# Two fused layers in f32: three d_ff chunks in a step of the inner loop, across block borders, in place of two

## The chip, the cores and the metric

The kernel runs on one core of one Trainium2 chip. The metric is device time in microseconds (us), the median of several executions; lower is better. Five engines work side by side, each through its own instructions in order, and wait for each other through semaphores: TensorE (PE, matrix multiplication), VectorE (DVE), ScalarE (ACT), GpSimd (POOL) and SyncE (SP, which issues the DMA transfers here). Matmul results land in PSUM, which has eight banks of 512 f32 columns on each of 128 partitions; all else lies in SBUF.

## The reference

Attention through 49 agent vectors, then a layer with two weight matrices, both on 4 batches of 12480 tokens with 128 channels, in f32.

```python
def _attn_ref(q, k, v, agents):
    scale = 1.0 / np.sqrt(q.shape[-1])
    def sm(a, b):
        s = scale * (a @ b.transpose(0, 2, 1))
        s = s - s.max(-1, keepdims=True)
        e = np.exp(s)
        return e / (e.sum(-1, keepdims=True) + 1e-09)
    agent_v = sm(agents, k) @ v
    return sm(q, agents) @ agent_v

def _moe_ref(x, w_in, w_out):        # w_in 128 x 2048, w_out 2048 x 128
    h = x @ w_in
    g = h - np.tanh(h)
    return g @ w_out
```

## The kernel before

**What it computes.** For each batch, *phase 1* forms `agent_v` from keys and values (scores, maxima, exponentials, sums) and multiplies it by `w_in`. The product, 49 agents by 2048, is kept as a high and a low part (`awh`, `awl`) in the type f32r, in which a matmul takes one pass; a plain f32 matmul takes four. After that a block of 480 tokens needs only its 49 softmax weights, also split into two parts and transposed (`pT`, 98 rows). For small h, h - tanh(h) is computed as h times the square of tanh(0.775 h) with a constant at the end; a general path stands behind a branch that is not taken on this data.

**The inner loop.** The work is 104 blocks of 480 tokens (26 a batch) by 16 chunks of 128 of the 2048 d_ff columns. A *step* is one block and two chunks, so there are 832:

- `m1` (L398, L399): four f32r matmuls of 480 columns on PE, which write h into a PSUM tile of two banks. There are three h tiles (six banks) and two single banks (`misc`) for everything else.
- `act`: on ACT tanh y from h (L408), its square z (L410); on DVE g = h * z (L412). Each works on 960 columns at once.
- `high` (L442): POOL copies g to gh in f32r, its high part. `low` (L447): DVE subtracts, gl = g - gh, the low part.
- `m2`: three f32r matmuls a chunk add into the block's output: gh with the low part of `w_out` (L459), gh with its high part (L460), gl with its high part (L461).

In every second block the last pair is *plain*: g itself is multiplied with f32 weights `wo_f` (L457), with neither gh nor gl. That is 52 pairs.

**The order.** The code issues m1 of step s, its `act` and `high`, `low` of step s-1 and `m2` of step s-2. A scheduler then sorts the instructions of each engine by a timeline of its own, within the dependencies, before the program is built; on the chip each engine keeps that order.

**Background.** Beside the loop run generators, advanced once a step: for every pair of blocks the softmax of the next pair (`q_softmax`: matmuls L353, DVE L363, L370 to L373, POOL L366 and L378, ACT L364, L368, L376) and two transposes (`q_transpose`, L385, L390); in the first three batches phase 1 of the next batch (matmuls L228, L276 and L327, DVE L232, L290, L331, L333, POOL L264, ACT L231, L266). Results leave through `finish` (L522). Before the loop, phase 1 of the first batch and the decoding of the weights run alone. In the main part keys go through three buffers and values through four.

Of the kernel before, what the change touches and what calls it, by code (L numbers as in the profile page):

```python
# [44 lines left out]
PCUT = (0, 256, 768, 1280, 1792, 2048)  # L45
NP = 5
KV0 = 13
KV = 3
VB = 4
PLAIN_PAIR = NCH // 2 - 1  # L50
PLAIN_EVERY = 2
LAG1 = 1
LAG2 = 1
NB = dict(y=2, z=2, g=4, gh=3, gl=2)
# [18 lines left out]
class Build:  # L73
    def __init__(self, ctx, tc, aps):
        self.tc, self.nc = tc, tc.nc
        self.qT, self.kT, self.v, self.agT, self.wi, self.wo, self.outT = aps
        self.pool = lambda name, bufs=1, **kw: tc.tile_pool(name=name, bufs=bufs, **kw)
        self.const = ctx.enter_context(self.pool("const"))
        self.keep = ctx.enter_context(self.pool("keep"))
        self.small = ctx.enter_context(self.pool("small", 2))  # L80
        self.ph = ctx.enter_context(self.pool("ph", 3, space=PSUM))
        self.pmisc = ctx.enter_context(self.pool("pmisc", 2, space=PSUM))

    def begin(self, ctx, name):
        self.work = ctx.enter_context(self.pool(name, reuse_waits="tile"))

    def wtile(self, tag, bufs):
        return self.work.tile([128, 1024], F32, tag=tag, name=tag, bufs=bufs)
# [4 lines left out]
    def constants(self):  # L93
# [15 lines left out]
        self.wo_f = c.tile([128, 2, C], F32, tag="wo_f", name="wo_f")  # L109
        self.vb = [c.tile([128, GT, C + 2], F32, tag=f"v{i}", name=f"v{i}") for i in range(VB)]  # L110
        for vt in self.vb:
# [39 lines left out]
    def load_w_out(self, c, raw):  # L151
# [7 lines left out]
        if c == PLAIN_PAIR // 2:  # L159
            nc.scalar.copy(self.wo_f.rearrange("p n e -> p (n e)"), w[:, 2 * C * (PLAIN_PAIR % 2) :][:, : 2 * C])  # L160

    def phase1(self, b):
        nc = self.nc
        st = {}
        kb, vb = (KV0 if b == 0 else KV), VB
# [7 lines left out]
        def load_k(g):  # L173
            n = tiles(g)
            kt = self.work.tile([128, GT * 128], F32, tag="kv", name="kt", bufs=kb)
            kt = kt.rearrange("p (t n) -> p t n", n=128)[:, :n, :]
# [3 lines left out]
        def load_v(g):  # L180
            vt = self.vb[g % VB]
# [13 lines left out]
        def scores(g):  # L195
# [7 lines left out]
            kt = ahead("k", load_k, g, kb if b == 0 else kb - 1)  # L203
            if b and g >= NG - vb:
                ahead("v", load_v, 0, g - NG + vb + 1)
            if b == 0:
                ps = self.ph.tile([128, 2, 512], F32, tag="h", name="h")
# [50 lines left out]
        def av(g):  # L258
            vt = ahead("v", load_v, g, vb - 1)
# [8 lines left out]
            if b == 0:  # L268
                if g == 0:
                    st["ps"] = self.ph.tile([128, 2, 512], F32, tag="h", name="h")[:, 0, :]  # L270
# [39 lines left out]
    def project(self, b, bound):  # L310
        nc = self.nc

        def part(c, lo, hi):
# [8 lines left out]
            if b == 0 and bound:  # L322
                ps = self.ph.tile([128, 2, 512], F32, tag="h", name="h")[:, 0, :]
# [69 lines left out]
    def m1(self, aw, pT, i):  # L393
        nc = self.nc
        h = self.ph.tile([128, 2, 512], F32, tag="h", name="h")
        for c in range(2):
            sl = slice((2 * i + c) * 128, (2 * i + c + 1) * 128)
            nc.tensor.matmul(h[:, c, :BLK], aw[0][:A2, sl], pT[:A2], start=True, stop=False)  # L398
            nc.tensor.matmul(h[:, c, :BLK], aw[1][:A2, sl], pT[:A2], start=False, stop=True)  # L399
        return h  # L400

    def pair(self, t):
        return t[:, : 2 * BLK].rearrange("p (c n) -> p c n", c=2)

    def act(self, h):
        nc = self.nc
        y = self.pair(self.wtile("y", NB["y"]))
        nc.scalar.activation(y, h[:, :, :BLK], AF.Tanh, scale=TSC)  # L408
        z = self.wtile("z", NB["z"])[:, : 2 * BLK]
        nc.scalar.activation(z, y.rearrange("p c n -> p (c n)"), AF.Square)  # L410
        g = self.wtile("g", NB["g"])[:, : 2 * BLK]
        nc.vector.tensor_tensor(self.pair(g), h[:, :, :BLK], self.pair(z), ALU.mult)  # L412
        return g

    def act_general(self, h):
        nc = self.nc
        hv = h[:, :, :BLK]
        d = self.wtile("y", NB["y"])[:, : 2 * BLK]
        u = self.wtile("z", NB["z"])[:, : 2 * BLK]
        nc.scalar.activation(self.pair(d), hv, AF.Tanh)  # L420
        nc.scalar.activation(self.pair(u), hv, AF.Square)
        nc.vector.tensor_tensor(self.pair(d), hv, self.pair(d), ALU.subtract)
        big = self.wtile("y", NB["y"])[:, : 2 * BLK]
        nc.vector.tensor_scalar(big, u, 4.0, None, ALU.is_ge)
        nc.vector.tensor_scalar(u, u, 16.0, None, ALU.min)
        r = self.wtile("z", NB["z"])[:, : 2 * BLK]
        nc.vector.tensor_scalar(r, u, 1.0 / 15.0, 13.0, ALU.mult, ALU.add)
        g = self.wtile("g", NB["g"])[:, : 2 * BLK]
# [7 lines left out]
        nc.vector.tensor_tensor(self.pair(g), hv, self.pair(g), ALU.mult)  # L436
# [3 lines left out]
    def high(self, g):  # L440
        gh = self.wtile("gh", NB["gh"])[:, : 2 * BLK].bitcast(F32R)
# [3 lines left out]
    def low(self, g, gh):  # L445
        gl = self.wtile("gl", NB["gl"])[:, : 2 * BLK].bitcast(F32R)
# [3 lines left out]
    def m2(self, acc, i, gh, gl):  # L450
        nc = self.nc
        for c in range(2):
            f = 2 * i + c
            x = slice(c * BLK, (c + 1) * BLK)
            first, last = f == 0, f == NCH - 1
            if gl is None:
                nc.tensor.matmul(acc[:, :BLK], self.wo_f[:, c, :], gh[:, x], start=first, stop=last)  # L457
                continue
            nc.tensor.matmul(acc[:, :BLK], self.wo_l[:, f, :], gh[:, x], start=first, stop=False)  # L459
            nc.tensor.matmul(acc[:, :BLK], self.wo_h[:, f, :], gh[:, x], start=False, stop=False)  # L460
            nc.tensor.matmul(acc[:, :BLK], self.wo_h[:, f, :], gl[:, x], start=False, stop=last)  # L461

    def fast(self):
        nc, tc = self.nc, self.tc
        HP = NCH // 2
        blocks = [(b, j) for b in range(B) for j in range(NBLK)]
        steps = [(n, i) for n in range(len(blocks)) for i in range(HP)]
# [58 lines left out]
        def foreground(n, i):  # L526
            h = self.m1(self.aw[blocks[n][0]], pT[n][0], i)
            while done:
                finish(done.pop(0))
            return h  # L530

        def rest(n, i, h):
            g = self.act(h)
            even = n % PLAIN_EVERY == 0
            plain = even and i == PLAIN_PAIR
            gh = None if plain else self.high(g)
            q1.append((n, i, g, gh))

        def low(keep):
            while len(q1) > keep:  # L540
                n, i, g, gh = q1.pop(0)
                q2.append((n, i, g, None) if gh is None else (n, i, gh, self.low(g, gh)))

        def out(keep):
            while len(q2) > keep:
                n, i, gh, gl = q2.pop(0)
                if i == 0:
                    acc[n] = self.misc()
                self.m2(acc[n], i, gh, gl)
                if i == HP - 1:  # L550
                    done.append(n)

        for n, i in steps:
            b = blocks[n][0]
            pos = (n % 2) * HP + i
            p = n // 2
            if n % NBLK == 0 and i == 0 and b + 1 < B:
                kq = self.phase1(b + 1)
            h = foreground(n, i)
            if n == 0 and i < len(rest0):  # L560
                run(rest0[i])
# [8 lines left out]
            rest(n, i, h)  # L570
            low(LAG1)
            out(LAG2)
# [9 lines left out]
            if (pos + 2) % 16 in KS and kq and n % NBLK < 25:  # L582
                start(kq.pop(0))
        low(0)
# [3 lines left out]
    def general(self):  # L588
# [10 lines left out]
        with tc.If(bits > HMAX_BITS):  # L599
            for b in range(B):  # L600
                for t in self.project(b, False):
                    run(t)
                with tc.For_i(0, NBLK * BLK, GW) as at:
                    pp = run_value(self.q_softmax, b, self.q_load(self.qT[:, ds(b * N + at, GW)]))
                    o = self.work.tile([128, GW], F32, tag="out", name="o", bufs=2)
                    for half in range(2):
                        pT = run_value(self.q_transpose, pp, half)
                        acc = self.misc()
                        for i in range(NCH // 2):
# [34 lines left out]
```

## Time and profile before

| | |
|---|---|
| median of three runs | 2228.51 us (2228.47 to 2228.87) |
| span of the profiled execution | 2226.8 us |
| instructions in the span | 31246 |
| first m1 matmul (L398) | 86.6 us after the start |
| first g (L412) | 92.3 us after the start |
| matmul pieces L398, L399 | 1664 each |
| L459, L460, L461 | 1560 each |
| steps with gh and gl (L442, L447) | 780 of 832 |

The times of the profile come from one execution, recorded on the chip. A row of a group of instructions reads: line, engine, operation, output <- inputs by the program's names with their shapes, count | busy us in all, mean ns of one | idle time of the engine just before them, with what ended most of it. A row of a timeline reads: start in us, duration in us, engine, line, operation, names, shapes, count; in square brackets the idle time ahead and what ended it. Adjacent rows of one kind are merged (x2). Recorded durations of neighbours on one engine overlap a little, since an instruction starts while the one before it still writes; the spacing of starts is what an operation costs. A row of a stretch reads: from and to, length, busy time of each engine (instructions), granted TensorE clock, busy share of the DMA engines, GB/s.

### The profile page before, as it was taken

To read this page: it belongs to the slowest core of one execution; us is meant where nothing else is said; L and a number is where in the kernel's file an instruction comes from. 1 tells how busy PE (TensorE), PEld (TensorE's weight loads), DVE (VectorE), ACT (ScalarE), POOL (GpSimd) and SP (SyncE) were. 2 spreads that over 40 slices of the span, in tenths; PEclk is the share of its full clock that TensorE was granted. 3 is DMA by queue.
4 is the path that set the end of the run, shared out by engine and by line. 5 is a ranking of instruction groups with operands and counts; after the bars stand their busy time and mean duration, and the time that the engine had idled before them with its cause. 6 is when DMAs were issued, how large, how long until landed. Compare 5 with 4: busy or idle time off the path is not lost.

```text
span 2226.8 us, 31246 instructions
## 1 busy us (share of the span) xinstructions
PE 2181.5 (98%) x11083; PEld 1838.3 (83%) x11083; DVE 2044.3 (92%) x2107; ACT 1812.7 (81%) x2179; POOL 1410.9 (63%) x957
## 2 busy tenths in 40 slices
PE   7699999999999999999999999999999999999998
PEld 7588878888888887888888888788888888888887
DVE  6998998889998999888999999988999999999998
ACT  3478887778887877877888878877889989898987
POOL 2555566656765647665666555766666767676776
PEclk9899999999999999999999999999999999999999
DMA  9411111211011110211011210121010000000000
GB/s 300 120 56 56 57 37 47 65 50 35 28 46 56 56 58 30 63 56 58 19 36 38 65 55 21 37 64 49 19 36 19 28 27 28 27 27 27 27 10 20
DMA packets 76658, 108.75 MB, mean 49 GB/s; under 512 B 4048, under 2 KB 56528, under 8 KB 76496
## 3 DMA queue, kind: packets, MB, share of 16 engines
q1 hardware_dynamic: 76496, 106.68, 15.1%
q8 instruction: 91, 1.49, 0.3%
q14 instruction: 71, 0.58, 0.1%
HBM read 81.10 MB, written 25.56 MB: 48 GB/s over the span
## 4 chain that ended last, share of the span: by engine, by line
PE 90%; DVE 5%; POOL 2%; issue 1%; ACT 1%; DMA 0%; POOLq 0%; SPq 0%; ACTq 0%; DVEq 0%
PE h L398 16%; PE h L399 15%; PE misc L461 15%; PE misc L459 14%; PE misc L460 14%; PE misc L457 4%; PE misc L353 4%; PE misc L276 3%; PE misc L228 3%; DVE gl L447 1%; DVE g L412 1%; POOL gh L442 1%; PE h L209 1%; PE misc L385 1%; PE misc L327 0%
## 5 line engine op out<-in xcount | busy, mean ns | idle before, releaser
L442 POOL TENSOR_SCALAR gh<-g 128x960 fp32r<-128x960 f32 x780 | 1201.8, 1542 | 636.1 <-DVE g L412 488.9
L447 DVE TENSOR_TENSOR gl<-g,gh 128x960 fp32r<-128x960 f32 x780 | 977.6, 1254 | 88.6 <-PE misc L461 62.3
L412 DVE TENSOR_TENSOR g<-h,z 128x960 f32<-128x960 f32 x832 | 950.9, 1147 | 55.7 <-ACT z L410 53.3
L408 ACT ACTIVATE y<-h 128x960 f32<-128x960 f32 x832 | 804.2, 971 | 214.1 <-PE h L399 207.6
L410 ACT ACTIVATE z<-y 128x960 f32<-128x960 f32 x832 | 832.5, 1007 | 24.8 <-DVE g L412 7.8
L398 PE MATMUL h<-pT,awh 98*128 98x480 f32 x1664 | 666.9, 401 | 1.8 <-DVE g L412 1.3
L399 PE MATMUL h<-pT,awl 98*128 98x480 f32 x1664 | 631.6, 380 | 0.0
L461 PE MATMUL misc<-gl,wo_h 128*128 128x480 f32 x1560 | 608.7, 390 | 3.9 <-DVE gl L447 3.8
L459 PE MATMUL misc<-gh,wo_l 128*128 128x480 f32 x1560 | 594.2, 381 | 3.8 <-POOL gh L442 3.6
L460 PE MATMUL misc<-gh,wo_h 128*128 128x480 f32 x1560 | 591.2, 379 | 0.0
L398 PEld LDWEIGHTS h<-pT,awh 98*128 98x128 f32 x1664 | 312.8, 188 | 65.3 <-issue 14.0
L399 PEld LDWEIGHTS h<-pT,awl 98*128 98x128 f32 x1664 | 314.5, 189 | 58.8 <-issue 11.9
L461 PEld LDWEIGHTS misc<-gl,wo_h 128*128 128x128 f32 x1560 | 292.4, 187 | 59.1 <-DVE gl L447 8.7
L459 PEld LDWEIGHTS misc<-gh,wo_l 128*128 128x128 f32 x1560 | 294.3, 189 | 54.0 <-POOL gh L442 11.1
L460 PEld LDWEIGHTS misc<-gh,wo_h 128*128 128x128 f32 x1560 | 292.9, 188 | 47.9 <-issue 0.2
L378 POOL TENSOR_TENSOR pp<-qe,pp 120x392 fp32r<-120x392 f32 x52 | 70.6, 1357 | 67.9 <-ACT pp L376 67.6
L353 PEld LDWEIGHTS misc<-ag,qt 128*120 128x120 f32 x832 | 96.8, 187 | 3.3
L353 PE MATMUL misc<-ag,qt 128*120 128x49 f32 x832 | 94.2, 267 | 0.0
L457 PE MATMUL misc<-g,wo_f 128*128 128x480 f32 x208 | 92.6, 567 | 0.0
L366 POOL TENSOR_TENSOR qe<-qe,qm 120x392 f32<-120x392 f32 x52 | 71.0, 1366 | 30.0 <-ACT qe L364 29.9
L522 ACT ACTIVATE o<-misc 128x480 f32<-128x480 f32 x104 | 58.7, 565 | 36.4 <-PE misc L457 22.8
L276 PEld LDWEIGHTS misc<-v,ke 128*49 128x49 f32 (+1 forms) x588 | 62.0, 123 | 17.5 <-issue 12.9
(85 smaller groups left out, 993.7 us busy)
## 6 DMA issues: line engine op xcount, KB each, us to landing
qt<-qT SPq DMA_DIRECT2D x52, 480.0 KB, 3.4
outT<-o SPq DMA_DIRECT2D x52, 480.0 KB, 2.6
kt<-kT SPq DMA_DIRECT2D x48, 512.0 KB, 3.6
v<-v SPq DMA_DIRECT2D x48, 512.0 KB, 4.1
raw<-w_in SPq DMA_DIRECT2D x4, 512.0 KB, 7.8
raw<-w_out SPq DMA_DIRECT2D x4, 512.0 KB, 9.5
kt<-kT SPq DMA_DIRECT2D x4, 128.0 KB, 2.0
v<-v SPq DMA_DIRECT2D x4, 64.0 KB, 1.9
```

Of the source, the lines that this page charges most:

```text
L353: nc.tensor.matmul(ps[:TT, t * A : (t + 1) * A], qt[:, t * TT : (t + 1) * TT], self.ag[:, b, :], start=True, stop=True)
L398: nc.tensor.matmul(h[:, c, :BLK], aw[0][:A2, sl], pT[:A2], start=True, stop=False)
L399: nc.tensor.matmul(h[:, c, :BLK], aw[1][:A2, sl], pT[:A2], start=False, stop=True)
L408: nc.scalar.activation(y, h[:, :, :BLK], AF.Tanh, scale=TSC)
L410: nc.scalar.activation(z, y.rearrange("p c n -> p (c n)"), AF.Square)
L412: nc.vector.tensor_tensor(self.pair(g), h[:, :, :BLK], self.pair(z), ALU.mult)
L442: self.nc.gpsimd.tensor_scalar(gh, g, 1.0, 0.0, ALU.mult, ALU.add)
L447: self.nc.vector.tensor_tensor(gl, g, gh.bitcast(F32), ALU.subtract)
L457: nc.tensor.matmul(acc[:, :BLK], self.wo_f[:, c, :], gh[:, x], start=first, stop=last)
L459: nc.tensor.matmul(acc[:, :BLK], self.wo_l[:, f, :], gh[:, x], start=first, stop=False)
L460: nc.tensor.matmul(acc[:, :BLK], self.wo_h[:, f, :], gh[:, x], start=False, stop=False)
L461: nc.tensor.matmul(acc[:, :BLK], self.wo_h[:, f, :], gl[:, x], start=False, stop=last)
```

## The change

- A step is three chunks. The loop walks the 104 x 16 = 1664 pairs (block, chunk) in order, three at a time, so that a step may hold chunks of two blocks; there are 555 steps, the last with two chunks. y, z, g, gh and gl are 1440 columns wide.
- An h tile has three PSUM banks, and there are two of them (six banks, as before).
- The square z is written into the tile of g, and g = h * z is formed in place. The tiles are now y 2, g 3, gh 4, gl 3 (before: y 2, z 2, g 4, gh 3, gl 2).
- No pair is plain: gh and gl are made for all 1664 chunks, and `wo_f` goes.
- Keys and values of batches 1 to 3 share five buffers in rotation.
- The background is advanced once for every even chunk in a step, once or twice a step; new jobs start at the same positions as before, counted in pairs of chunks.
- The first cut of the first batch's projection has 384 columns in place of 256 (and the second as many fewer).

The general path behind the branch is changed in the same way; it is left out here.

```diff
-PCUT = (0, 256, 768, 1280, 1792, 2048)
+PCUT = (0, 384, 768, 1280, 1792, 2048)
-KV = 3
-VB = 4
-PLAIN_PAIR = NCH // 2 - 1
-PLAIN_EVERY = 2
+RB = 5
+HP = NCH // 2
+W = 3
-NB = dict(y=2, z=2, g=4, gh=3, gl=2)
+NB = dict(y=2, g=3, gh=4, gl=3)
...
-        self.ph = ctx.enter_context(self.pool("ph", 3, space=PSUM))
+        self.ph = ctx.enter_context(self.pool("ph", 2, space=PSUM))
...
+    def wtile(self, tag, w):
+        return self.work.tile([128, W * BLK], F32, tag=tag, name=tag, bufs=NB[tag])[:, : w * BLK]
+
+    def htile(self):
+        return self.ph.tile([128, W, 512], F32, tag="h", name="h")
+
+    def slot(self):
+        self.nslot += 1
+        return self.kvb[self.nslot % RB]
...
+                kt = self.slot()[:, :n, :C]
...
-            vt = self.vb[g % VB]
+            vt = self.slot()
...
+    def m1(self, items, pT):
+        nc = self.nc
+        h = self.htile()
+        for c, (n, f) in enumerate(items):
+            awh, awl = self.aw[n // NBLK]
+            sl = slice(f * 128, (f + 1) * 128)
+            nc.tensor.matmul(h[:, c, :BLK], awh[:A2, sl], pT[n][0][:A2], start=True, stop=False)
+            nc.tensor.matmul(h[:, c, :BLK], awl[:A2, sl], pT[n][0][:A2], start=False, stop=True)
+        return h[:, : len(items), :BLK]
...
     def act(self, h):
         nc = self.nc
-        y = self.pair(self.wtile("y", NB["y"]))
-        nc.scalar.activation(y, h[:, :, :BLK], AF.Tanh, scale=TSC)
-        z = self.wtile("z", NB["z"])[:, : 2 * BLK]
-        nc.scalar.activation(z, y.rearrange("p c n -> p (c n)"), AF.Square)
-        g = self.wtile("g", NB["g"])[:, : 2 * BLK]
-        nc.vector.tensor_tensor(self.pair(g), h[:, :, :BLK], self.pair(z), ALU.mult)
+        w = h.shape[1]
+        y = self.split(self.wtile("y", w))
+        g = self.wtile("g", w)
+        gv = self.split(g)
+        nc.scalar.activation(y, h, AF.Tanh, scale=TSC)
+        nc.scalar.activation(gv, y, AF.Square)
+        nc.vector.tensor_tensor(gv, h, gv, ALU.mult)
         return g
...
+        for at in range(0, len(items), W):
+            its = items[at : at + W]
+            h = self.m1(its, pT)
+            while done:
+                finish(done.pop(0))
+            steps = [(n, f // 2) for n, f in its if f % 2 == 0]
+            for n, i in steps:
+                b = n // NBLK
+                if n % NBLK == 0 and i == 0 and b + 1 < B:
+                    kq = self.phase1(b + 1)
+                if n == 0 and i < len(rest0):
+                    run(rest0[i])
+                advance()
+                if n != steps[-1][0] or i != steps[-1][1]:
+                    begin(n, i)
+            g = self.act(h)
+            q1.append((its, g, self.high(g)))
+            low(LAG1)
+            out(LAG2)
+            if steps:
+                begin(*steps[-1])
```

The scheduler sorts the new program anew. On DVE, in a stretch of the last batch without background, the rows before read as follows (the numbers behind a name tell the tiles of one name apart; a larger one was made later):

```order
L412 TENSOR_TENSOR g_18547<-h_18536,z_18545 128x960
L447 TENSOR_TENSOR gl_18551<-g_18519,gh_18521 128x960
L412 TENSOR_TENSOR g_18568<-h_18559,z_18566 128x960
L447 TENSOR_TENSOR gl_18572<-g_18547,gh_18549 128x960
L412 TENSOR_TENSOR g_18589<-h_18580,z_18587 128x960
L447 TENSOR_TENSOR gl_18593<-g_18568,gh_18570 128x960
```

In the changed program, in which L420 makes g and L451 makes gl, DVE's rows in a stretch of the last batch are:

```order
L420 TENSOR_TENSOR g_15620<-h_15607,g_15620 128x1440
L420 TENSOR_TENSOR g_15647<-h_15637,g_15647 128x1440
L451 TENSOR_TENSOR gl_15653<-g_15620,gh_15624 128x1440
L451 TENSOR_TENSOR gl_15679<-g_15647,gh_15651 128x1440
L420 TENSOR_TENSOR g_15673<-h_15664,g_15673 128x1440
L420 TENSOR_TENSOR g_15701<-h_15691,g_15701 128x1440
```

Before, g and gl alternate, and a gl belongs to the step before that of the g ahead of it (gl_18572 reads g_18547, while g_18568 stands between). Now two g are followed by the two gl of the same two steps. Of the 555 steps 542 stand in such groups of four; a few near the borders of batches are ordered otherwise.

On PE, in the same stretches, the rows before are m1 of one step, then matmuls of the step four earlier, then m1 again:

```order
L398 MATMUL h_18536<-pT_18285,awh_15307 128x480
L399 MATMUL h_18536<-pT_18285,awl_15308 128x480
L398 MATMUL h_18536<-pT_18285,awh_15307 128x480
L399 MATMUL h_18536<-pT_18285,awl_15308 128x480
L461 MATMUL misc_18461<-gl_18481,wo_h_84 128x480
L459 MATMUL misc_18461<-gh_18457,wo_l_85 128x480
L460 MATMUL misc_18461<-gh_18457,wo_h_84 128x480
L461 MATMUL misc_18461<-gl_18481,wo_h_84 128x480
L459 MATMUL misc_18461<-gh_18479,wo_l_85 128x480
L460 MATMUL misc_18461<-gh_18479,wo_h_84 128x480
L398 MATMUL h_18559<-pT_18285,awh_15307 128x480
```

In the changed program L405 and L406 are m1, L457 and L458 multiply gh, L459 multiplies gl:

```order
L406 MATMUL h_15607<-pT_15519,awl_13022 128x480
L457 MATMUL misc_15533<-gh_15568,wo_l_85 128x480
L458 MATMUL misc_15533<-gh_15568,wo_h_84 128x480
L405 MATMUL h_15637<-pT_15519,awh_13021 128x480
L406 MATMUL h_15637<-pT_15519,awl_13022 128x480
L405 MATMUL h_15637<-pT_15519,awh_13021 128x480
L406 MATMUL h_15637<-pT_15519,awl_13022 128x480
L405 MATMUL h_15637<-pT_15519,awh_13021 128x480
L406 MATMUL h_15637<-pT_15519,awl_13022 128x480
L459 MATMUL misc_15533<-gl_15596,wo_h_84 128x480
L457 MATMUL misc_15533<-gh_15568,wo_l_85 128x480
L458 MATMUL misc_15533<-gh_15568,wo_h_84 128x480
```

Two m1 now stand close together, with only two matmuls of the step two earlier between them; the first matmul that reads gl follows the second m1, and behind it come the remaining seven matmuls of that step and all nine of the next.

136 lines of the change are left out of this document (50 added, 86 removed).

## The prediction

> **What bounds the kernel now.** I read the page first: the busy shares, then the chain that ended last, then the groups of instructions.
>
> ```profile
> PE 2181.5 (98%) x11083; PEld 1838.3 (83%) x11083; DVE 2044.3 (92%) x2107; ACT 1812.7 (81%) x2179; POOL 1410.9 (63%) x957
> PE 90%; DVE 5%; POOL 2%; issue 1%; ACT 1%; DMA 0%; POOLq 0%; SPq 0%; ACTq 0%; DVEq 0%
> L442 POOL TENSOR_SCALAR gh<-g 128x960 fp32r<-128x960 f32 x780 | 1201.8, 1542 | 636.1 <-DVE g L412 488.9
> L447 DVE TENSOR_TENSOR gl<-g,gh 128x960 fp32r<-128x960 f32 x780 | 977.6, 1254 | 88.6 <-PE misc L461 62.3
> L412 DVE TENSOR_TENSOR g<-h,z 128x960 f32<-128x960 f32 x832 | 950.9, 1147 | 55.7 <-ACT z L410 53.3
> L408 ACT ACTIVATE y<-h 128x960 f32<-128x960 f32 x832 | 804.2, 971 | 214.1 <-PE h L399 207.6
> L410 ACT ACTIVATE z<-y 128x960 f32<-128x960 f32 x832 | 832.5, 1007 | 24.8 <-DVE g L412 7.8
> ```
>
> TensorE (PE) holds 90% of the last chain and VectorE (DVE) is busy 92%: two engines close together, so the order in which they hand work over matters as much as the amounts. Next I cut the span by stage, and count one step by its multiplication g (L412).
>
> ```profile
> 120.00:1720.00 1600.00, 696.03 (x610) 1.00 0.15 45
> 1740.00:2200.00 460.00, 223.63 (x196) 1.00 0.07 24
> 120.00:1720.00 1600.00, 1593.44 (x8115) 1338.71 (x8114) 1469.20 (x1496) 1315.68 (x1576) 1001.79 (x686) 1.00 0.15 45
> 1740.00:2200.00 460.00, 460.00 (x2222) 388.94 (x2221) 443.14 (x440) 413.54 (x476) 330.12 (x207) 1.00 0.07 24
> ```
>
> The first two rows are of L412 alone, the last two of all engines (PE first). Three steps of two chunks are six chunks, as many as two steps of the new loop; I call this a **double step**. It takes 3 x 1600/610 = 7.87 us in the first three batches, whose background computes the next batch's attention, and 3 x 460/196 = 7.04 us in the last. PE is idle in neither.
>
> Now a quiet place of the last batch, DVE rows and then GpSimd (POOL) rows:
>
> ```profile
> 1916.98 1.14 DVE L412 TENSOR_TENSOR g<-h,z 128x960 f32<-128x960 f32 x1
> 1918.05 1.14 DVE L447 TENSOR_TENSOR gl<-g,gh 128x960 fp32r<-128x960 f32 x1
> 1919.11 1.14 DVE L412 TENSOR_TENSOR g<-h,z 128x960 f32<-128x960 f32 x1
> 1920.18 1.14 DVE L447 TENSOR_TENSOR gl<-g,gh 128x960 fp32r<-128x960 f32 x1
> 1918.30 1.75 POOL L442 TENSOR_SCALAR gh<-g 128x960 fp32r<-128x960 f32 x1 [0.39 <-DVE g L412]
> 1920.43 1.75 POOL L442 TENSOR_SCALAR gh<-g 128x960 fp32r<-128x960 f32 x1 [0.39 <-DVE g L412]
> ```
>
> DVE starts an operation every 1.067 us and alternates g, gl. The copy gh that starts at 1918.30, inside a gl, takes 1.75 us. Compare one of the few places where the old order has g, g, gl, gl:
>
> ```profile
> 206.42 2.22 DVE L412 TENSOR_TENSOR g<-h,z 128x960 f32<-128x960 f32 x2 [1.12 <-ACT z L410]
> 208.56 0.55 DVE L232 TENSOR_REDUCE mxp<-misc 128x49 f32<-128x392 f32 x1
> 209.03 2.86 DVE L447 TENSOR_TENSOR gl<-g,gh 128x960 fp32r<-128x960 f32 x2
> 207.74 2.09 POOL L442 TENSOR_SCALAR gh<-g 128x960 fp32r<-128x960 f32 x2 [3.63 <-DVE g L412]
> ```
>
> Here two copies take 2.09 us, about 1.0 each: they ran beside g and the reduction. The two gl, issued at 209.03, end at 211.89, and 211.89 - 209.83 (the end of the second copy) is 2.06, room for two of them and no more. So **gh and gl exclude each other**: a copy loses about 0.75 us inside a gl, and a gl issued during a copy waits for its end. g does not disturb a copy.
>
> The Trainium skill says the same (SBUF — State Buffer, "Who interferes with whom"): a DVE instruction with two SBUF inputs contends with a GpSimd instruction that reads SBUF, one with at most one SBUF input does not, and issue order decides who blocks. The trace agrees: gl reads g and gh in SBUF, 1.75 against 1.0 us; g has h in PSUM.
>
> **The change part by part.**
>
> *Plain pairs go.*
>
> ```profile
> 2202.55 1.77 PE L457 MATMUL misc<-g,wo_f 128*128 128x480 f32 x4
> 2203.78 0.76 PE L398 MATMUL h<-pT,awh 98*128 98x480 f32 x1
> 1917.18 0.38 PE L399 MATMUL h<-pT,awl 98*128 98x480 f32 x1
> 1917.40 0.38 PE L398 MATMUL h<-pT,awh 98*128 98x480 f32 x1
> ```
>
> 52 pairs lose their four f32 passes, 0.4 us each: the matmul behind them starts at 2203.78 but ends at 2204.54, so its own 0.38 began at 2204.16, which is 1.6 after 2202.55. Six matmuls at a spacing of 0.22 us (1917.18 to 1917.40) replace them, 1.3. PE gains 52 x 0.3 = 15.6 us, or 0.06 in each of 277 double steps; POOL and DVE get 52 more pairs to split, priced next.
>
> *Wider operations.* From 392 columns (0.47 us from 208.56 to 209.03) and 960 (1.067) a column costs 0.00105 us, so 1440 cost 1.57; in proportion it would be 1.60, with all cost fixed 1.07, and I take 1.57. DVE then needs 555 x 2 x 1.57 = 1743 us for g and gl, against (832 + 780) x 1.067 = 1720 before: the 52 extra pairs eat what the width saves. For a copy gh I take 1.0 x 1.5 = 1.5 us; the lower end is 1.3, from a small POOL row as if its time were fixed (0.4 + 0.6 x 1.5):
>
> ```profile
> L264 POOL TENSOR_TENSOR ke<-s,mb 128x98 f32<-128x98 f32 x3 | 1.2, 397 | 0.2
> L522 ACT ACTIVATE o<-misc 128x480 f32<-128x480 f32 x104 | 58.7, 565 | 36.4 <-PE misc L457 22.8
> ```
>
> For ScalarE (ACT), 0.565 at 480 columns and 0.971 at 960 give y 1.38 and z 1.41; four of them are 5.6 us a double step, below PE.
>
> *The order.* In the new order DVE does g, g, gl, gl in nearly all of the 277 double steps, where before it alternated; PE does m1(s), two matmuls of step s-2, m1(s+1), then the rest of s-2 and s-1. The two copies follow their g, and the second cannot start before the second g has ended. The place at 206.42 prices this at 960 columns. From 206.42 to 211.82 (the last gl's start, 210.75, and one spacing of 1.067) are 5.40 us; four operations are 4.27, so 1.13 are lost: the second copy (1.0) and its hand-over. The reduction lies inside that gap and costs nothing. At 1440 columns: 4 x 1.57 + 1.13 + 0.5 (the longer copy) = **7.91 us**. If the first gl wins instead, the second copy runs between the two gl, at the same price. Behind the gl that waits stand the next two g on DVE; m1 of the step after next waits for them to give back h, and behind it all of PE's queue. 7.91 is above PE's 7.87 - 0.06 = 7.81, and far above its 7.04 - 0.06 = 6.98 in the last batch: what only covered becomes the bound.
>
> *Background beside it.*
>
> ```profile
> L373 DVE TENSOR_TENSOR qe<-qe,qs 120x392 f32<-120x392 f32 x52 | 34.0, 655 | 0.6
> L363 DVE TENSOR_REDUCE qm<-misc 120x8 f32<-120x392 f32 x52 | 29.0, 559 | 3.2 <-PE misc L353 1.7
> L370 DVE TENSOR_REDUCE qs<-qe 120x8 f32<-120x392 f32 x52 | 28.4, 546 | 1.3 <-ACT qe L368 1.3
> L232 DVE TENSOR_REDUCE mxp<-misc 128x49 f32<-128x392 f32 x36 | 20.0, 556 | 0.6 <-ACT s L231 0.6
> L371 DVE TENSOR_SCALAR qs<-qs 120x8 f32<-120x8 f32 x52 | 10.6, 205 | 0.1
> L333 DVE TENSOR_REDUCE mx<-awh 49x1 f32<-49x512 f32 x15 | 10.0, 666 | 0.0
> L372 DVE RECIPROCAL qs<-qs 120x8 f32<-120x8 f32 x52 | 9.9, 190 | 0.2
> L290 DVE TENSOR_TENSOR acc<-acc,misc 49x129 f32<-49x129 f32 x36 | 9.8, 273 | 0.4
> L366 POOL TENSOR_TENSOR qe<-qe,qm 120x392 f32<-120x392 f32 x52 | 71.0, 1366 | 30.0 <-ACT qe L364 29.9
> L378 POOL TENSOR_TENSOR pp<-qe,pp 120x392 fp32r<-120x392 f32 x52 | 70.6, 1357 | 67.9 <-ACT pp L376 67.6
> L264 POOL TENSOR_TENSOR ke<-s,mb 128x392 f32<-128x392 f32 x36 | 37.6, 1049 | 22.7 <-PE misc L276 22.4
> ```
>
> The DVE rows sum to 152 us, 0.55 a double step; in the new order about half of them stand where DVE waits anyway, between g and gl or between two gl, so 0.3 count (0 to 0.55). The POOL rows sum to 179 us, 0.65 a double step; they too exclude gl, or stand ahead of a copy. I count a little under half, 0.3 (0 to 0.65). Forecast: 7.91 + 0.3 + 0.3 = **8.5 us**.
>
> *At nothing:* z written into g and multiplied in place (DVE still reads one SBUF operand; bounds nothing to one spacing more, and only three g tiles: z(s+5) needs gl(s+2), which ends 6.3 us into DVE's round at the latest, 7.91 - 1.57, and by B's path below it starts at 7.1); keys and values in five shared slots (DMA is busy 0.15 of the stretch; a load that came late would hold PE's background matmuls and all behind them, and no row shows one); two h tiles instead of three: m1(s+2) needs g(s), done about 1.6 us into DVE's round, while PE still has seven matmuls (1.5 us) of step s-1. The start may move by 0 to 3 us: the first projection is 384 columns, and the first batch's scores have two tiles.
>
> *The sum.*
>
> ```profile
> L412 DVE TENSOR_TENSOR g<-h,z x832: 1094/1146/1159, 92.3 to 2215.8; 128x960 f32<-128x960 f32 x167
> ```
>
> The first g starts at 92.3, and from the last one to the span's end at 2226.8 are 11.0 us. 92.3 + 277.5 x 8.5 + 11.0 = 2462. The median of the runs, 2228.51, is 1.7 above the profiled span: **2464 us**.
>
> **The rivals.** *A, the bare loop:* all background hides; 7.91 gives 92.3 + 2195 + 11 + 1.7 = 2300 us. For it: the reduction at 208.56 cost nothing. Against: DVE's small rows stand largely between two g.
>
> *B, the way back through PE and ACT decides.* From the end of a gl: seven matmuls and m1 (13 x 0.22 = 2.9), four serial ACT operations (5.6), then g, the copy and two gl (1.57 + 1.63 + 3.14 = 6.3), hand-overs 0.6: 15.4 us, and that spans two double steps, 7.7 each, just under the loop. With one double step's background on it (PE 7.87 - 30 x 0.22 = 1.3; ACT (1315.68 - 610 x 1.978)/203 = 0.5; DVE 0.55) it is 17.8, or 8.9 a double step in three batches; in the last, with PE's 7.04 - 6.6 = 0.4 and some 0.8 of the others, 8.3: 208 x 8.9 + 69.5 x 8.3 + 105 = 2533 us. For it: only two h tiles. Against: the order puts many background matmuls ahead of a matmul that waits for gl.
>
> *C, faster.* The copy does not stay exposed, because POOL and DVE interleave otherwise at this width. DVE's round is then 6.28 + 0.55 = 6.83, below PE's 7.81 and 6.98; PE stays the bound and gains its 15.6: 2228.5 - 15.6 = 2213 us. It decides where less than about 0.9 us of the copy is exposed. For it: calm stretches of before lose nothing to the exclusion. Against: those alternate g and gl, which the new order does not. The Trainium skill (Perfetto Trace Analysis, "Optimizing Scalar/DVE Operations") would lean this way: grouping into larger operations can improve the throughput of a saturated engine, since each pays a fixed overhead. The trace agrees as far as the 1.57 against 1.60 above, which is 0.03 an operation.
>
> **How the numbers follow.** Forecast 0.55, A 0.17, B 0.18, C 0.10. The range, 2285 to 2580, takes in A, the forecast with a copy of 1.3 us (8.3, 2408 us), and B with a fifth more background on its path (9.1, about 2580); it leaves out C. A run can tell about 0.2% from no change: faster by more 0.07, within 0.03 (C with a dearer start), slower 0.90.
>
> **What would show it.** Right: DVE rows come as g x2, gl x2; two copies of about 1.5 us where they meet g; gl's mean far above 1.6; PE busy near 90%; the chain goes through gl and gh. B: long waits of g for z, and of ACT for PE. Wrong, towards C: PE still 98% busy, gl near 1.6. I am wrong in size if a double step is not 8.2 to 8.8 us.

## The result, and the profile after

The changed kernel takes **2441.04 us** (2440.32 to 2443.52, four runs) against 2228.49 (2228.28 to 2228.87) before: a ratio of 1.0953, 95% interval 1.0938 to 1.0969. The prediction was 2464 us. The profiled execution's span is 2439.6 us.

From the page of the changed kernel: the engines' busy time, the shares of the chain that ended last, and the three groups of DVE and POOL that the loop consists of (L420 makes g, L446 gh, L451 gl).

```profile
PE 2255.6 (92%) x11187; PEld 1836.1 (75%) x11187; DVE 2069.6 (85%) x1605; ACT 1731.9 (71%) x1624; POOL 1301.0 (53%) x733
PE 29%; DVE 27%; POOL 19%; ACT 13%; issue 10%; DMA 0%; POOLq 0%; DVEq 0%; SPq 0%; ACTq 0%
L446 POOL TENSOR_SCALAR gh<-g 128x1440 fp32r<-128x1440 f32 x555 | 1100.7, 1983 | 917.5 <-DVE g L420 829.9
L451 DVE TENSOR_TENSOR gl<-g,gh 128x1440 fp32r<-128x1440 f32 x555 | 972.9, 1755 | 275.4 <-POOL gh L446 270.8
L420 DVE TENSOR_TENSOR g<-h,g 128x1440 f32<-128x1440 f32 x555 | 904.5, 1648 | 48.9 <-ACT g L419 47.8
```

PE had 90% of the chain and has 29%; DVE and POOL have 46% together, yet no engine is busier than 92%. That is the picture of a loop of hand-overs, not of a full engine. DVE stood idle 270.8 us ahead of gl for the copy gh; the kernel before had 88.6 us of idle time ahead of gl, most of it for PE. The waits of the changed kernel, in all, times and longest:

```profile
DVE gl L451 <- POOL gh L446: 270.8, 236, 2.2
PEld misc L459 <- DVE gl L451: 164.9, 188, 2.1
PE misc L459 <- DVE gl L451: 93.6, 134, 1.7
```

236 waits in 277 double steps are nearly one in each, and PE waits for gl in its turn. The starts of g in two stretches, DVE's rows of L420 alone, inside the first three batches and inside the last:

```profile
120.00:1840.00 1720.00, 661.64 (x405) 1.00 0.14 43
1900.00:2400.00 500.00, 198.05 (x123) 1.00 0.06 21
```

A double step takes 2 x 1720/405 = 8.49 us (7.87 before) and 2 x 500/123 = 8.13 (7.04). In a quiet place of the last batch, DVE's and then POOL's timeline:

```profile
2105.60 3.21 DVE L420 TENSOR_TENSOR g<-h,g 128x1440 f32<-128x1440 f32 x2
2108.84 1.66 DVE L451 TENSOR_TENSOR gl<-g,gh 128x1440 fp32r<-128x1440 f32 x1
2111.79 1.66 DVE L451 TENSOR_TENSOR gl<-g,gh 128x1440 fp32r<-128x1440 f32 x1 [1.30 <-POOL gh L446]
2113.37 3.21 DVE L420 TENSOR_TENSOR g<-h,g 128x1440 f32<-128x1440 f32 x2
2107.40 1.40 POOL L446 TENSOR_SCALAR gh<-g 128x1440 fp32r<-128x1440 f32 x1 [3.41 <-DVE g L420]
2108.97 2.79 POOL L446 TENSOR_SCALAR gh<-g 128x1440 fp32r<-128x1440 f32 x1 [0.17 <-DVE g L420]
```

The bare loop is 2113.37 - 2105.60 = 7.77 us. The first copy runs beside the second g and takes 1.40. The second is issued at 2108.97, after the first gl (2108.84), and takes 2.79: it waits for that gl and then runs alone, while DVE stands idle 1.30 us ahead of the second gl. That hole comes back in every pair of steps without background. (The first gl is held a little too: it starts 2108.84 - 2105.60 = 3.24 us after the first g, where two spacings of 1.57 would be 3.14, and the first copy ends at 2107.40 + 1.40 = 2108.80.)

The start came later too. From the chains that ended last, a stretch of the kernel before and then of the changed one (start, duration, what):

```profile
82.81 1.74 DVE rem L134
84.96 1.19 PE h L327 x2
86.60 0.77 PE h L398
```

```profile
82.24 3.36 PE misc L359 x16
85.61 1.36 PE h L333 x2
87.37 3.52 PE misc L234 x16
90.89 0.53 PE h L405
```

The first m1 went from 86.60 to 90.89: in the new order of PE two groups of 16 background matmuls (the softmax of the next pair of blocks, and the next batch's scores) stand ahead of it.

### The profile page after: what moved, and what is told of

Its sections match the earlier page's. It is cut to its first block, busy times and chain, and to the rows that moved or that the text cites. A ratio compares the mean times of both kernels' runs of the same rounds, so it can differ in the third digit from the quotient of the medians.

```text
span 2439.6 us, 28847 instructions
## 1 busy us (share of the span) xinstructions
PE 2255.6 (92%) x11187; PEld 1836.1 (75%) x11187; DVE 2069.6 (85%) x1605; ACT 1731.9 (71%) x1624; POOL 1301.0 (53%) x733
## 4 chain that ended last, share of the span: by engine, by line
PE 29%; DVE 27%; POOL 19%; ACT 13%; issue 10%; DMA 0%; POOLq 0%; DVEq 0%; SPq 0%; ACTq 0%
POOL gh L446 18%; DVE g L420 17%; DVE gl L451 6%; ACT g L419 6%; ACT y L418 6%; PE misc L459 5%; PE h L405 4%; PE misc L457 4%; PE h L406 4%; PE misc L458 4%; PE misc L359 2%; PE misc L282 2%; PE misc L234 1%; PE h L215 1%; DVE qe L379 1%
## 5 line engine op out<-in xcount | busy, mean ns | idle before, releaser
L446 POOL TENSOR_SCALAR gh<-g 128x1440 fp32r<-128x1440 f32 x555 | 1100.7, 1983 | 917.5 <-DVE g L420 829.9
L451 DVE TENSOR_TENSOR gl<-g,gh 128x1440 fp32r<-128x1440 f32 x555 | 972.9, 1755 | 275.4 <-POOL gh L446 270.8
L418 ACT ACTIVATE y<-h 128x1440 f32<-128x1440 f32 x555 | 759.7, 1369 | 475.2 <-PE h L406 475.2
L420 DVE TENSOR_TENSOR g<-h,g 128x1440 f32<-128x1440 f32 x555 | 904.5, 1648 | 48.9 <-ACT g L419 47.8
L419 ACT ACTIVATE g<-y 128x1440 f32<-128x1440 f32 x555 | 782.1, 1409 | 12.2
L459 PE MATMUL misc<-gl,wo_h 128*128 128x480 f32 x1664 | 649.6, 397 | 94.8 <-DVE gl L451 93.6
L457 PE MATMUL misc<-gh,wo_l 128*128 128x480 f32 x1664 | 655.3, 394 | 35.4 <-POOL gh L446 34.6
L405 PE MATMUL h<-pT,awh 98*128 98x480 f32 x1664 | 649.9, 391 | 15.6 <-DVE g L420 14.8
L458 PE MATMUL misc<-gh,wo_h 128*128 128x480 f32 x1664 | 633.2, 381 | 0.0
L406 PE MATMUL h<-pT,awl 98*128 98x480 f32 x1664 | 632.2, 380 | 0.0
L459 PEld LDWEIGHTS misc<-gl,wo_h 128*128 128x128 f32 x1664 | 313.1, 188 | 214.1 <-DVE gl L451 164.9
L457 PEld LDWEIGHTS misc<-gh,wo_l 128*128 128x128 f32 x1664 | 314.6, 189 | 124.2 <-POOL gh L446 83.3
L405 PEld LDWEIGHTS h<-pT,awh 98*128 98x128 f32 x1664 | 313.1, 188 | 96.6 <-DVE g L420 43.0
L406 PEld LDWEIGHTS h<-pT,awl 98*128 98x128 f32 x1664 | 314.2, 189 | 44.1 <-issue 0.2
L458 PEld LDWEIGHTS misc<-gh,wo_h 128*128 128x128 f32 x1664 | 314.6, 189 | 42.9 <-issue 0.8
L234 PEld LDWEIGHTS misc<-ag,v 128*128 128x128 f32 x588 | 73.9, 196 | 4.2 <-ACT qe L370 1.6
L282 PE MATMUL misc<-v,ke 128*49 128x129 f32 (+1 forms) x588 | 74.0, 276 | 2.5 <-ACT qe L370 2.5
```

The costliest lines, as they stand in the source:

```text
L282: nc.tensor.matmul(ps[:A, : C + 1], e3[:r, t, :], vt[:r, t, : C + 1], start=(first and t == 0), stop=(last and t == n - 1),)
L405: nc.tensor.matmul(h[:, c, :BLK], awh[:A2, sl], pT[n][0][:A2], start=True, stop=False)
L406: nc.tensor.matmul(h[:, c, :BLK], awl[:A2, sl], pT[n][0][:A2], start=False, stop=True)
L418: nc.scalar.activation(y, h, AF.Tanh, scale=TSC)
L419: nc.scalar.activation(gv, y, AF.Square)
L420: nc.vector.tensor_tensor(gv, h, gv, ALU.mult)
```

## The experiments

Twelve kernels ran. The theory: **two h tiles** lead to the order g, g, gl, gl, and in that order the **exclusion** of gh and gl lays a copy bare. The rivals: that the way from gl back to g over PE and ACT decides (B of the prediction), that fewer g tiles or z in place cost the time, or that the missing plain pairs do. A difference to a kernel with one run has no interval. All runs in one table; the double steps are worked out from the starts of g, as a mean of the first three batches and for the last.

| kernel | us | ratio, 95% interval | double step |
|---|---|---|---|
| before | 2228.5 | 1 | 7.87, 7.04 |
| after | 2441.0 | 1.0953 (1.0938 to 1.0969) | 8.51, 8.12 |
| e1: after, g and gl alternate | 2332.4 | 1.0466 (1.0449 to 1.0484) | 8.14, 7.69 |
| e2: after, gh without reading | 2281.4 | one run | 8.00, 7.35 |
| e5: both | 2242.1 | one run | 7.88, 7.16 |
| e6: e1, m2 a step later | 2305.9 | 1.0344 (1.0327 to 1.0362) | 8.09, 7.45 |
| e9: after, a third of the copy on ACT | 2390.7 | one run | 8.33, 7.93 |
| e3: after, two chunks, three h tiles | 2256.0 | 1.0125 (1.0108 to 1.0142) | 7.93, 7.29 |
| e8: e3 with five g tiles | 2260.1 | 1.0141 (1.0124 to 1.0158) | 7.97, 7.21 |
| e4: e3 with two h tiles | 2605.2 | one run | 9.11, 8.78 |
| e7: before without plain pairs | 2259.8 | 1.0141 (1.0124 to 1.0158) | 7.94, 7.29 |
| e10: e3 alternating, m2 later | 2233.8 | 1.0024 (1.0014 to 1.0033) | 7.85, 7.13 |
| e11: e10, every fourth copy on ACT | 2247.5 | 1.0085 (1.0069 to 1.0102) | 7.88, 7.25 |
| e12: e10 with plain pairs | 2246.0 | 1.0077 (1.0064 to 1.0091) | 7.87, 7.22 |

### The order (e1)

A dependency that orders but adds no semaphore ties each g and gl to the one before it in the code's sequence, so that DVE does g(s), gl(s-1), g(s+1), gl(s). The scheduler sorts the other engines anew around it: on PE the two m1 that stood close together in the changed kernel come apart, and six matmuls of m1 and nine of m2 mostly take turns.

```diff
-        nc.vector.tensor_tensor(gv, h, gv, ALU.mult)
+        self.order(nc.vector.tensor_tensor(gv, h, gv, ALU.mult))
-        self.nc.vector.tensor_tensor(gl, g, gh.bitcast(F32), ALU.subtract)
+        self.order(self.nc.vector.tensor_tensor(gl, g, gh.bitcast(F32), ALU.subtract))
```

> The changed kernel with one thing added: VectorE's g and gl are bound to the alternating order g(s), gl(s-1), g(s+1), gl(s) by order-only edges; width, two h tiles and all sizes stay. Theory 1 (a copy and a gl exclude each other, and the order g, g, gl, gl lays one copy bare): nothing is laid bare, VectorE's round is 4 x 1.57 + 0.55 = 6.8 us a double step, TensorE bounds again with 7.8 and 7.0, 2215 to 2280 us, and gl waits less than 60 us for gh (271 in the changed kernel). Theory 2 (the way back through two h tiles, TensorE and four serial ScalarE operations bounds, whatever VectorE's order): 2400 us or more, with g waiting for z.

Groups of instructions of e1, in which L457 makes gh, L462 gl and L431 g:

```profile
L457 POOL TENSOR_SCALAR gh<-g 128x1440 fp32r<-128x1440 f32 x555 | 1440.9, 2597 | 543.3 <-DVE g L431 532.7 <-POOL qe L372 4.8 <-DVE qs L377 1.5
L462 DVE TENSOR_TENSOR gl<-g,gh 128x1440 fp32r<-128x1440 f32 x555 | 942.5, 1698 | 6.4 <-POOL gh L457 6.4
L431 DVE TENSOR_TENSOR g<-h,g 128x1440 f32<-128x1440 f32 x555 | 916.0, 1650 | 208.3 <-ACT g L430 203.9
```

DVE's wait for gh falls from 270.8 to 6.4 us and the time by 109. The order is a cause (DVE's and the order of PE that came with it; the two were not separated), but only half of the loss comes back, and the time lies between the ranges of both theories. Nearly every copy now lies behind a gl (mean 2.60 us, from 1.98), PE waits 77.4 + 49.6 us for gh (weight loads and matmuls), and g waits 203.9 us for z. The last looks like B's signature; e5 below shows that it is not what costs the rest.

### The exclusion alone (e2), and both (e5)

POOL fills gh with a constant after g is done, instead of copying g. The high part of the product is left out, and g - gh is no longer the low part; the number of instructions and what each waits for stay, and DVE's order stays grouped (273 groups of g, g, gl, gl; 271 in the changed kernel).

```diff
-        self.nc.gpsimd.tensor_scalar(gh, g, 1.0, 0.0, ALU.mult, ALU.add)
+        m = self.nc.gpsimd.memset(gh.bitcast(F32), 0.5)
+        self.tc.add_manual_dep(
+            m.ins,
+            self.gi.name,
+            mybir.DependencyInfo(mybir.DependencyClass.Sync, mybir.DependencyReason.DATA),
+            reason="after g",
+        )
```

> The changed kernel, in which GpSimd fills gh with a constant in place of copying g into it; it still waits for g, and all orders stay (g, g, gl, gl). This leaves the high part out of the computation. Theory 1 in its narrow form (what excludes gl is GpSimd's reading of SBUF): the fill runs beside gl, the second gl follows the first without a gap, 2215 to 2290 us. Theory 1 in a wide form (any GpSimd instruction in SBUF excludes gl): the gap stays as long as the fill, 2350 to 2440 us. Theory 2 (two h tiles): near 2440 us.

> e1 and e2 together: g and gl alternate, and GpSimd fills gh with a constant (the high part is left out of the computation). e1 alone left 2332 us, e2 alone 2281. Theory 1 says that both act on one loss, the copy laid bare, so together they give hardly more than e2: 2240 to 2285 us. Theory 1 with a second cause in e1 (under alternation the exclusion still stretches a copy from 1.40 to 2.67 us, and with two h tiles there is no slack for it): e1's rest goes as well, 2215 to 2250 us. Theory 2 (two h tiles bound by themselves): 2280 us or more, with g waiting for z over 200 us as in e1 and e2.

Groups of e2 (L449 fills gh, L460 makes gl):

```profile
L420 DVE TENSOR_TENSOR g<-h,g 128x1440 f32<-128x1440 f32 x555 | 915.9, 1652 | 228.6 <-ACT g L419 225.0
L460 DVE TENSOR_TENSOR gl<-g,gh 128x1440 fp32r<-128x1440 f32 x555 | 906.5, 1659 | 8.0 <-POOL gh L449 8.0
L449 POOL MEMSET gh<- 128x1440 f32 x555 | 723.2, 1303 | 1079.9 <-DVE g L420 1010.6 <-DVE qs L378 48.4 <-DVE qs L377 10.3
```

In the same order as after, gl takes 1.66 us beside POOL's work and waits 8.0 us in all; 160 us of the 212 lost are gone. A pure change of duration does not explain it: the fill takes 1.30 us, the undisturbed copy 1.40. This is the statement of the Trainium skill (SBUF — State Buffer, "Who interferes with whom") that a DVE instruction with two SBUF inputs contends with a GpSimd instruction that reads SBUF and not with one that only writes it; the trace agrees, with 1.66 us for gl here and 1.76 in the changed kernel. With the order changed as well, 2242.1 us are left, a time inside the ranges of both forms of theory 1. Against e1 only the fill is new, and DVE, ACT and nearly all of PE keep e1's order: g still waits 194.3 us for z (203.9 in e1), but PE's waits for gh fall from 77.4 + 49.6 to 7.7 + 2.1 us, and those of m1 for g from 38.0 + 23.7 to 16.6 + 5.9. So the rest of e1's loss hangs on the stretched copies, not on the wait for z by itself. The two causes overlap: the exclusion costs 160 us in the grouped order and 2332.4 - 2242.1 = 90 in the alternating one; the order costs 109 us with the exclusion and 39 without.

### The tiles (e3, e4, e8)

e3 sets the step back to two chunks with three h tiles and keeps the rest; e4 takes away one h tile from that; e8 gives e3 five g tiles.

```diff
-W = 3
+W = 2
...
-        self.ph = ctx.enter_context(self.pool("ph", 2, space=PSUM))
+        self.ph = ctx.enter_context(self.pool("ph", 3, space=PSUM))
```

> The changed kernel with steps of two chunks and three h tiles as before; the plain pairs stay out, z is formed in g's tile, and keys and values share the five slots. VectorE's order alternates again for most of the program. Theory 1: TensorE bounds, the plain pairs' 15.6 us are won, and the few places with g, g, gl, gl cost some 1 us each: 2205 to 2240 us. Rival (without the plain pairs VectorE, at 2.13 us a step for 52 more pairs, becomes the bound): 2250 us or more.

> As e3, but with two h tiles instead of three. The scheduler then sets VectorE's order to g, g, gl, gl nearly throughout, at 960 columns. Theory 1: two steps cost 5.40 us as at 206.42 in the kernel before, and 0.2 to 0.4 of background: 416 x 5.6 to 5.8 + 105 = 2430 to 2520 us, slower than three chunks. Rival (the width of 1440 is to blame, with its longer hand-overs): like e3, 2205 to 2260 us.

> e3 (two chunks, three h tiles) with five g tiles instead of three. In e3 ScalarE waits 64 us for gl before it may write z into a g tile, which the kernel before did not do. If this costs e3 its 28 us: 2210 to 2235 us. If the missing plain pairs do: 2250 us or more.

The third chunk with its two h tiles costs 2441.0 - 2256.0 = 185 us. e3 itself came out where its rival had put it, 27.5 us above the kernel before; e7 below says why. The number of g tiles is not a cause: 2260.1 with five against 2256.0 with three. e4 came out above its expected range. It has nothing of the wide step and only one h tile less than e3, and the scheduler sets g, g, gl, gl for it nearly throughout. DVE in the last batch of e4:

```profile
2104.12 2.21 DVE L420 TENSOR_TENSOR g<-h,g 128x960 f32<-128x960 f32 x2
2106.46 1.16 DVE L451 TENSOR_TENSOR gl<-g,gh 128x960 fp32r<-128x960 f32 x1
2108.50 1.16 DVE L451 TENSOR_TENSOR gl<-g,gh 128x960 fp32r<-128x960 f32 x1 [0.89 <-POOL gh L446]
2109.58 1.15 DVE L420 TENSOR_TENSOR g<-h,g 128x960 f32<-128x960 f32 x1
2111.62 1.16 DVE L420 TENSOR_TENSOR g<-h,g 128x960 f32<-128x960 f32 x1 [0.90 <-ACT g L419]
2112.70 1.15 DVE L451 TENSOR_TENSOR gl<-g,gh 128x960 fp32r<-128x960 f32 x1
2114.74 1.16 DVE L451 TENSOR_TENSOR gl<-g,gh 128x960 fp32r<-128x960 f32 x1 [0.89 <-POOL gh L446]
2115.81 2.22 DVE L420 TENSOR_TENSOR g<-h,g 128x960 f32<-128x960 f32 x2
```

The first group of four takes 2109.58 - 2104.12 = 5.46 us, near the 5.40 that the prediction read off the place at 206.42. The next takes 6.23, because its second g also waits 0.90 for z. Six chunks are one and a half such groups: 8.19 us at the first price alone, and 8.78 were measured in the last batch. Waits for z make up part of the difference: in the last batch they come in 25 of 104 groups, 22.4 us in all, or 0.32 a double step; the rest stands beside background. So two h tiles bring the order, and the wide step then softens it: one hole of 1.30 for six chunks, against one of 0.89 for four.

### What is left of after when g and gl alternate (e6, e9)

e6 adds to e1 that the matmuls of m2 come one step later (`LAG2 = 2`, ordered behind the next m1). e9 leaves the order of after, but lets ACT copy the third chunk:

```diff
+        w = min(g.shape[1], 2 * BLK)
-        self.nc.gpsimd.tensor_scalar(gh, g, 1.0, 0.0, ALU.mult, ALU.add)
+        self.nc.gpsimd.tensor_scalar(gh[:, :w], g[:, :w], 1.0, 0.0, ALU.mult, ALU.add)
+        if w < g.shape[1]:
+            self.nc.scalar.copy(gh[:, w:], g[:, w:])
```

> e1, with m2 of a step queued on TensorE behind m1 of the step three later by order-only edges (LAG2 = 2), so that no matmul that waits for gh stands ahead of the next m1. In e1 TensorE waits 127 us for gh. If that wait is what holds up m1 and so z and g: 2230 to 2280 us and g waits for z under 100 us (204 in e1). If the two h tiles hold m1 up anyway (it waits for g): 2310 us or more.

> The changed kernel; GpSimd copies two of a step's three chunks into gh and ScalarE the third. The order stays g, g, gl, gl. If the laid-bare copy sets the pace, its length sets the time: 1.40 us becomes about 0.97, so 0.43 less in each of 277 double steps, 2441 - 119 = 2322 us, up to 2370 with ScalarE's 555 added copies of 0.56 us now and then late. If the length of the copy does not matter (only that gl waits for another engine's hand-over): 2430 us or more.

e6 wins 26 us over e1 and falls between its two expected ranges: PE waits 20.0 + 11.3 us for gh in place of 77.4 + 49.6, but g still waits 181.1 us for z (203.9 in e1), and m1 now waits 76.0 + 48.2 us for g to give back an h tile. What one wait gave up, the others took in part. That the two h tiles bound e6 is not shown: e5 has no more of them and takes 2242.1. e9 missed its expected range on the dear side. DVE's rows of e9 (L454 makes gl):

```profile
2108.90 1.65 DVE L454 TENSOR_TENSOR gl<-g,gh 128x1440 fp32r<-128x1440 f32 x1
2111.44 1.66 DVE L454 TENSOR_TENSOR gl<-g,gh 128x1440 fp32r<-128x1440 f32 x1 [0.89 <-POOL gh L447]
2113.02 1.65 DVE L420 TENSOR_TENSOR g<-h,g 128x1440 f32<-128x1440 f32 x1
2114.89 1.66 DVE L420 TENSOR_TENSOR g<-h,g 128x1440 f32<-128x1440 f32 x1 [0.22 <-ACT g L419]
```

The hole ahead of the second gl shrinks from 1.30 to 0.89, as a shorter copy should make it. But a hole of 0.22 opens ahead of the second g, now that the copies take their turn on ACT among the squares: g waits 122.1 us for z in all, 47.8 in after.

### The plain pairs, and a version near both (e7, e10, e11, e12)

e7 is the kernel before with `plain = False`. e10 is e3 with g and gl alternating, m2(s) behind m1(s+4), and five g, six gh and four gl tiles. e11 gives every fourth copy of e10 to ACT. e12 is e10 with the plain pairs and the first cut of 256 columns of the kernel before.

```diff
-            plain = even and i == PLAIN_PAIR
+            plain = False
```

> The kernel before with one edit: no pair is plain. The prediction's term says that TensorE gains 15.6 us and the added gh and gl are covered: 2208 to 2222 us. Rival, after e3's 2256 us: the plain pairs relieved VectorE and GpSimd once in every sixteen steps, and without them the order has no slack: 2240 us or more, and e3 is explained by this alone.

> e3 (two chunks, three h tiles, no plain pairs) with g and gl alternating everywhere, m2 of a step behind m1 of the step four later on TensorE, and g 5, gh 6, gl 4 tiles. If the missing plain pairs cost e3 and e7 their 28 to 31 us through places with g, g, gl, gl and through waits for late copies, these go and TensorE's floor is near: 2212 to 2232 us. If VectorE, held up by the copies, is simply full (busy 95% in e7): 2245 us or more.

> e10, with every fourth copy gh made by ScalarE in place of GpSimd. ScalarE gets 208 us more (busy 81% in e7), and a quarter of the collisions between gh and gl go. If the exclusion fills VectorE up: some 25 to 40 us below e10, or at TensorE's floor, 2212 to 2225 us. If it does not: like e10, or slower by ScalarE's added work.

> The ordered kernel of two chunks with three h tiles (2233.79 us, 7.85 us a double step in the first three batches and 7.13 in the last), with the 52 plain pairs of the kernel before put back and the first cut of the projection at 256 columns again. Two things are asked. The start: if the cut makes the 4.4 us by which the first g came later, the first g is at 92.3 again; if the slots or the tiles do, it stays near 96.6. The plain pairs: the prediction took PE as the bound and 0.3 us more of PE for each of them. If that holds where the order no longer loses time, a double step grows by 0.06, 7.91 and 7.19, and the time is 2233.8 + 15.6 = 2249 us, 2245 with the earlier start. If plain pairs still relieve DVE and POOL more than they cost PE, as in the kernel before without them (+31 us), the double step falls below 7.85 and 7.13, and the time lies at 2210 to 2225 us, below both kernels. If PE's queue alone sets the pace, as in the kernel before, 7.87 and 7.04: 2228 us.

DVE and PE busy in e7, and its group of gl:

```profile
PE 2188.1 (97%) x11187; PEld 1848.3 (82%) x11187; DVE 2139.8 (95%) x2159; ACT 1817.5 (81%) x2179; POOL 1522.6 (67%) x1009
L447 DVE TENSOR_TENSOR gl<-g,gh 128x960 fp32r<-128x960 f32 x832 | 1069.8, 1287 | 76.0 <-PE misc L461 45.9 <-POOL gh L442 17.0 <-POOL pp L378 4.9
```

Without plain pairs the kernel before gets 31 us slower: DVE is busy 95.5 us more, 92.2 of them in gl, which has 52 more instructions and a mean of 1.29 us for 1.25. The 31 us account for the loss of e3 (27.5), so z in place, shared slots and three g tiles together cost nothing that shows. In e10 the same pairs are missing and the loss is 5.3 us, just above the expected range; its later start (first g at 96.66, before at 92.35) alone is 4.3. In e12 the sign turns: put back into e10 (with the old first cut), the pairs cost 2246.0 - 2233.8 = 12.2 us. That sum is near the 15.6 by which PE should lose, but it does not lie where the expectation put it: a double step grows by 0.03 in the first three batches and by 0.09 in the last, where 0.06 was expected in both. **The same plain pairs are worth 31 us in the order of the kernel before and cost 12 in that of e10; why the sign turns is not shown.** The reading that they cost wherever PE is the bound does not fit: they cost most in the last batch, and there, from 1740 to 2200 us of e10, DVE is the engine that never stops (460.0 us busy, PE 455.1). e11 is slower than e10 by 13.7 us: g waits for z 91.8 us for 71.8, as in e9. No version tried beats the kernel before; e10 comes nearest, at 1.0024. What keeps the last batch of e12 at 7.22 us, where the kernel before has 7.04 with the same instructions on PE, was not settled.

## Why the prediction was right

**The mechanism** held: DVE issues g, g, gl, gl, the second copy cannot hide, and the chain goes over DVE and POOL. It said that if the first gl wins, the second copy runs between the two gl at the same price; that is what the quiet place shows. e1 and e2 show each half of it as a cause, by 109 and 160 us. Two of its signs came otherwise, because the first gl wins: one copy of each pair takes 2.79 us in place of about 1.5, and gl's mean is 1.76, not far above 1.6; the loss shows as idle time ahead of gl.

**The bare loop** was 7.91 and is 7.77. The width was right (1.58 us from a gl to the next g, and 3.24 for two g less the 0.10 that the first gl is held, against 1.57 each); the copy was put at 1.5 and takes 1.40, and of the 1.63 that a pair of steps should lose, 1.49 are lost.

**The background** was 0.6 us a double step. It is 8.49 - 7.77 = 0.72 in three batches and 8.13 - 7.77 = 0.36 in the last, 0.63 on average, if all that exceeds the bare loop is called background. The last batch lacks the attention of a next one, which the prediction did not tell apart; its 8.13 lies just below the 8.2 to 8.8 that were forecast. So it was partly luck that the mean came out near 0.6: the two parts are off in opposite directions.

**The sum.** From the first to the last g are 2330.9 us in place of 277.5 x 8.5 = 2359, which is 28 less. The start (first g at 96.55 in place of 92.3) and the tail (12.1 for 11.0) take back 5. That is the distance from 2464 to 2441.

**The start** had been given 0 to 3 us and counted as nothing; it was 4.2. It is neither the two h tiles nor the cut: e4 has both, and its first g is at 90.8; e12, with three h tiles and the old cut, has 95.8. What goes with it is where the scheduler puts the background's matmuls on PE, as the rows above show: from 70 to 92 us PE runs 15 matmuls before and in e3 (first g at 91.1), 42 in after and 43 in e12.

**Two h tiles at nothing** was right as a wait: in after, g waits only 47.8 us for z, so B did not decide. But e4 shows that it is the missing tile that brings the grouped order, which the prediction took from the program without asking what had set it. In e1, e2 and e5 g waits 194 to 225 us for z, as B has it; how much time that costs was not measured, and e5, with 194 of it, is within 14 us of the kernel before.

**Plain pairs** had a PE term of -15.6 us, used in C alone. e12 has a sum near it (12.2), spread otherwise than the term says. In the old order the same edit costs 31 us (e7), with 92 us more of gl on DVE, work that the prediction had only set against the gain of width. C would have failed even without the exclusion: e5 is at 2242, not 2213.

**C's argument from width** drew on the Trainium skill (Perfetto Trace Analysis, "Optimizing Scalar/DVE Operations"). The same section says that where Scalar or Vector is not saturated but causes bubbles on other engines, breaking instructions up may let work complete sooner. Here DVE fell from 92% to 85% busy while PE came to wait for gl, but no run bears that rule out by itself: the return from three chunks to two won 185 us together with a third h tile (e3), and with two h tiles the narrower instructions took 2605.2 - 2441.0 = 164 us more than the wide ones (e4). One h tile less and nothing else, e4 against e3, is 2605.2 - 2256.0 = 349 us.

## What to carry to other kernels

A wider operation is paid for with tiles; count what order the remaining tiles allow before counting what the width saves. Two engines that exclude each other on a pair of operations must have something else to do in between, so the order of their instructions is part of the cost: a change of order was worth 109 us here, the width some 0.03 us an operation. And the worth of a relief such as a plain f32 pair belongs to one order: the same pairs won 31 us in one and lost 12 in another, so measure it again when the order changes.

## What the hardware showed beside it

TensorE dropped to half its clock after a short pause. In e1, the windows of PE around a wait of 1.23 us for gh (busy time, granted clock), and PE's timeline:

```profile
2101.00:2102.30 1.30, 0.07 (x2) 0.89 0.00 0
2102.30:2105.30 3.00, 3.00 (x8) 0.50 0.00 0
```

```profile
2100.69 0.37 PE L406 MATMUL h<-pT,awl 98*128 98x480 f32 x1
2102.29 0.77 PE L468 MATMUL misc<-gh,wo_l 128*128 128x480 f32 x1 [1.23 <-POOL gh L457]
2102.86 0.60 PE L469 MATMUL misc<-gh,wo_h 128*128 128x480 f32 x1
2103.26 0.60 PE L470 MATMUL misc<-gl,wo_h 128*128 128x480 f32 x1
```

For 3.0 us the matmuls start every 0.40 us and not every 0.22, at a granted clock of 0.50. It is rare: behind the first 120 us and up to the tail e1 has 26 pauses of PE of over 1.0 us and four such stretches, each with one of these pauses in the 3.4 us ahead of it; the longest pause, 2.10 us, has none behind it. Here PE was busy 1.84 of the 3.41 us before the clock fell (2098.62 to 2102.03); a shorter pause of 0.60 lies there too. One stretch costs about 8 x (0.40 - 0.22) = 1.4 us. The Trainium skill (TensorE: Matmul & The Clock Gate, "Part 1: The HAM clock gate (the "warmup" mystery)") gives half clock after an idle window of about 3.4 us. The trace differs: this pause was a third of that, and the measurement decides.
